# Moving a block's last transpose and its stores behind the next block's first two seed sums on VectorE

## Chip, cores, metric

One NeuronCore of one Trainium2 chip. The metric is the device time of one execution in microseconds (us), median over the runs; lower is better.

## The reference, cut to what matters

```python
# attention part: a causal convolution of 7 taps along the sequence, weights per head
out = np.einsum('hk,bskhg->bshg', w, x_unf)       # B=8, S=4096, D=192
# MoE part, on x = out as (32768, 192)
h = x @ w_in                                      # (32768, 2048)
g = h * np.clip(h + 3.0, 0.0, 6.0) / 6.0
return (g @ w_out).astype(np.float32)             # (32768, 192)
```

## The kernel before

The tokens are worked in 32 blocks of 1024. Both matmuls are done by a Strassen scheme (7 products in place of 8) with float32 operands. Blocks 1 to 31 each have an *h phase* (y times w_in, line 311) and an *out phase* (g times w_out, L422 before, L427 after the change). Matmuls are queued without a break between the two. In the h phase, two independent units L and U run side by side in rows 0 to 63 and 64 to 127 of the array ("halves" below). A list of steps, PLAN, says in which order one pair of units and the pair before it are worked; an apostrophe marks the pair before.

```python
    PLAN = """
        LP1 LRd' UP1 LGd' LP4' UP4' URd' LF1 LP5 UGd' UF1 UP5 LP6 UP6 LP2 LCE UCE LRb'
        UK11 LAF UAF LK11 URb' UP2 LP7 LGb' UP7 LK12 UP3 UGb' LAD LP3 LRa URa LRf UK12
        UAD UGa LGa LK22 UK22 URf LGf UGf LK21 UK21
    """.split()
    # ... in Unit.run(op): P*, K* are matmuls; R is a relu on ScalarE; G a gate on VectorE
            elif op == "F1":                       # ScalarE: bank b starts as a copy of a
                bank["b"] = take()
                nc.scalar.copy(out=psum[:, bank["b"]], in_=psum[:, bank["a"]])
            elif op == "CE":                       # ScalarE: product 5 to SBUF
                self.p5 = p5s.tile([P, N], F32, name="p5")
                nc.scalar.copy(out=self.p5[:], in_=psum[:, bank["e"]])
                give(bank["e"])
            elif op in ("AF", "AD"):               # VectorE: the "seed sums", L391
                to = bank[op[1].lower()] = take()
                nc.vector.tensor_tensor(
                    out=psum[:, to], in0=psum[:, bank["b"]], in1=self.p5[:], op=ALU.add
                )
```

AF reads bank b after product P6 has been added to it, and P7 is added to the same bank afterwards. So P7 has to wait for AF. The out phase ends with sums on VectorE, each followed by a transpose and stores:

```python
        # ... end of out_strassen(i, conv)
        b, bank = three(3, 5, 2)
        piece(p5, 2, bank, NQ)                     # ScalarE copy
        add(u2[:], u2[:], bank[m])                 # VectorE
        give(b)
        add(u2[:], u2[:], p5[:])
        store(i, u2, 0, 1)                         # VectorE transpose, three stores on SyncE
        add(u3[:], u3[:], p5[:])
        store(i, u3, 1, 1)
        # ... main loop: h_phase(); out_strassen(i, ...); x_tiles[i + 2] = load_x(i + 2)
```

Of the kernel before, what the change touches and what calls it, by code (L numbers as in the profile page):

```python
# [16 lines left out]
def kernel(  # L17
# [33 lines left out]
    K3 = D // D2  # L51
# [197 lines left out]
    def conv_units(i, parts, cuts=1):  # L249


        x = x_tiles.pop(i)
        W = N // cuts

        def tap(part, k, t):
            c = c_sb[:, k : k + 1]
            to = y[:, part, t : t + W]
            if k == 0:
                nc.vector.tensor_scalar(  # L259
                    out=to, in0=x[:, part, t : t + W], scalar1=c, scalar2=None, op0=ALU.mult  # L260
                )
            else:
                nc.vector.scalar_tensor_tensor(  # L263
                    out=to, in0=x[:, part, k + t : k + t + W], scalar=c, in1=to,
                    op0=ALU.mult, op1=ALU.add,
                )

        return [
            lambda part=part, k=k, t=t: tap(part, k, t)
            for part in parts for k in range(KC) for t in range(0, N, W)  # L270
        ]
# [28 lines left out]
    def give(b):  # L300
        free_banks.append(b)
# [32 lines left out]
    def h_out(c, group, bs, between):  # L334
# [10 lines left out]



    PLAN = """
        LP1 LRd' UP1 LGd' LP4' UP4' URd' LF1 LP5 UGd' UF1 UP5 LP6 UP6 LP2 LCE UCE LRb'
        UK11 LAF UAF LK11 URb' UP2 LP7 LGb' UP7 LK12 UP3 UGb' LAD LP3 LRa URa LRf UK12  # L350
        UAD UGa LGa LK22 UK22 URf LGf UGf LK21 UK21
    """.split()

# [46 lines left out]
                gate(g_of(2 * u + c, group, k), self.r6[op[1]][:], psum[:, b])  # L400
                give(b)

    def h_phase():
        last = None
        for u in range(UNITS + 1):
            now = [Unit(u, k) for k in range(2)] if u < UNITS else None
            for step in PLAN:
                which = last if step[-1] == "'" else now
                if which:
                    which["LU".index(step[0])].run(step[1:].rstrip("'"))  # L410
            if last:
                g_sums(nc.gpsimd, (1, 3), range(2 * u - 2, 2 * u), 2)
            last = now
# [58 lines left out]
    def g_sums(engine, which, slots, width):  # L472

        forms = {
            1: (S1, A21, A22, ALU.add), 3: (S3, A11, A21, ALU.subtract),
            2: (S2, S1, A11, ALU.subtract), 4: (S4, A12, S2, ALU.subtract),
        }
# [50 lines left out]
    def store(i, c, k, half_, qs=range(NQ), queues=(nc.sync,)):  # L528

        xt = ot.tile([P, N], F32, name="xt")  # L530
        r = slice(qs[0] * QS, (qs[-1] + 1) * QS)
        nc.vector.transpose(out=xt[r], in_=c[r])  # L532
        for q in qs:
            store_rows(i, k, half_ * NQ + q, xt, q, queues[q % len(queues)])
# [46 lines left out]
    def out_strassen(i, conv):  # L581
        p1, p2, p4, p5, u2, u3 = sums_tiles()
        for u in conv:
            u()
        b, bank = three(1, 2, 0)
        nc.scalar.copy(out=p1[:], in_=bank[m])  # L586
        piece(p2, 0, bank, NQ)
        give(b)
        g_sums(nc.vector, (2,), every, 4)
        b, bank = three(4, 2, 1)  # L590
        nc.scalar.copy(out=p4[:], in_=bank[m])  # L591
        piece(p2, 1, bank, NQ)
        give(b)
        swap(slice(0, K3))
        b, bank = by_quarters(2, 2)
        pieces(p2, 2, bank)
        give(b)
        g_sums(nc.vector, (4,), every, 4)
        add(p2[:], p1[:], p2[:])
        store(i, p2, 0, 0)  # L600
        b7, bank7 = three(7, 5, 0)
        piece(p5, 0, bank7, NQ)
        y_sums()
        b, bank = three(6, 5, 1)
        piece(p5, 1, bank, NQ)
        add(u2[:], p1[:], bank[m])
        give(b)
        add(u3[:], u2[:], bank7[m])
        give(b7)
        add(p4[:], u3[:], p4[:], ALU.subtract)  # L610
        store(i, p4, 1, 0)
        b, bank = three(3, 5, 2)
        piece(p5, 2, bank, NQ)
        add(u2[:], u2[:], bank[m])
        give(b)
        add(u2[:], u2[:], p5[:])
        store(i, u2, 0, 1)
        add(u3[:], u3[:], p5[:])
        store(i, u3, 1, 1)

    def split(n):
        if n < len(units):
# [15 lines left out]
    with tc.manual_schedule():  # L638
        nc.vector.tensor_reduce(out=sm[:], in_=e_sb[:], axis=AX.X, op=ALU.add)
        nc.vector.tensor_scalar_add(sm[:], sm[:], 1e-9)  # L640
        nc.vector.reciprocal(sm[:], sm[:])
        nc.vector.tensor_tensor(
            out=c_sb[:], in0=e_sb[:], in1=sm[:].to_broadcast([P, KC]), op=ALU.mult
        )

        thirds = [slice(s, s + 1) for s in range(K3)]
        pe_third = K3 - 1
        b = take()
        for _ in range(3):

            nc.tensor.matmul(
                out=psum[:, b], lhsT=zeros[:, 0:P], rhs=zeros[:], start=True, stop=True
            )
        for k in range(KC):
            nc.scalar.mul(diag[:, k], ident[:], c_sb[:, k : k + 1])
            nc.tensor.matmul(
                out=psum[:, b], lhsT=diag[:, k], rhs=x_tiles[0][:, pe_third, k : k + N],
                start=(k == 0), stop=(k == KC - 1),
            )
        conv0 = conv_units(0, thirds[:pe_third], 2)  # L660
        per = len(conv0) // pe_third
        for k, u in enumerate(conv0):
            if k == 5:
                split(0)
                clamp(0)
            elif k == per - 3:
                join(0, more=False)
            elif k == per:
                nc.scalar.copy(out=y[:, pe_third], in_=psum[:, b])
                give(b)  # L670
                swap(thirds[0])
                swap(thirds[pe_third])
                load(AHEAD)
                split(1)
                clamp(1)
            elif k == per + 6:
                split(2)
                join(1)
                clamp(2)
            u()  # L680
        swap(thirds[1])
        split(3)
        split(4)
        join(2)
        clamp(3)


        parts = [(c, group) for p in range(0, NP, 2) for group in (OWN, OTHER)
                 for c in (p, p + 1)]
        early = [(c, group, (take(), take())) for c, group in parts[:4]]  # L690
        order = (0, pe_third, 1)
        for c in range(2):
            for slot, group, bs in early:
                if slot == c:
                    for s in order[:2]:
                        h_mm(c, group, bs, s, order)
        for c, group, bs in early:
            h_mm(c, group, bs, order[2], order)

        slots = [0, 1, 2, 3, 5, 6, 8, 10, 12, 14]  # L700
        n = 3
        for slot, (c, group) in enumerate(parts):
            first = slot < len(early)
            if first:
                bs = early[slot][2]
            else:
                bs = take(), take()
                for s in range(K3):
                    h_mm(c, group, bs, s)
            more = slot in slots  # L710

            def between():
                if more:
                    join(n)
                    clamp(n + 1)

            if slot == 6:
                x_tiles[1] = load_x(1)
            h_out(c, group, bs, (lambda: None) if first else between)
            if more:  # L720
                split(n + 2)
                if first:
                    between()
                n += 1
        while n < len(units):
            join(n)
            clamp(n + 1)
            split(n + 2)
            n += 1
        w_sums()  # L730
        start_pools.close()
        ss = ctx.enter_context(tc.tile_pool(name="ss", bufs=1))
        p5s = ctx.enter_context(tc.tile_pool(name="p5s", bufs=3))
        cs = ctx.enter_context(tc.tile_pool(name="cs", bufs=1))
        ot = ctx.enter_context(tc.tile_pool(name="ot", bufs=4))

        def conv_and_swap(i):
            return conv_units(i, [slice(0, K3)]) + [lambda: swap(slice(0, K3)), y_sums]

        out_direct(0, conv_and_swap(1))  # L740
        x_tiles[2] = load_x(2)

        S1 = ss.tile([P, NP, N], F32, name="s1")[:]
        for i in range(1, NB):
            h_phase()
            if i + 1 < NB:
                out_strassen(i, conv_units(i + 1, [slice(0, K3)]))
            else:
                out_last(i)
            if i + 2 < NB:  # L750
                x_tiles[i + 2] = load_x(i + 2)
# [33 lines left out]
```

## Time and profile before

| | before |
|---|---|
| time, median (range), 6 runs | 2442.48 us (2442.38 to 2442.60) |
| profiled span | 2440.7 us |
| h phases, first / 23 of them / 7 of them | 38.52 / 39.12 / 39.16 us |
| out phases | 36.19 us |
| transpose of 96x512 on VectorE | 0.708 us, 123 times |

A profile line of a group gives line, engine, operation, shapes and count, then busy time and mean duration in ns, then the engine's idle time ahead of the group and what ended most of it. The waits give who waited for whom: total us, times, longest. The two lines that belong to the seed sums, from the groups of the page and from the list of waits:

```profile
L391 DVE TENSOR_TENSOR psum<-psum,p 128x512 f32<-128x512 f32 x496 | 320.9, 693 | 208.7 <-PE psum L311 204.1
```
```profile
PEld psum L311 <- DVE psum L391: 26.7, 68, 0.6
```

By the first, VectorE mostly waits for TensorE there, not the other way round. The second shows the exceptions: 68 weight loads, about two per block, were released by a seed sum. The rest is read in the prediction.

### The profile page before, as it was taken

The page shows a single profiled execution, that of the slowest core. Times are in us where ns is not written, and L with a number is a line of the kernel's source. Part 1 is how long each engine was busy: PE and PEld are TensorE (multiplying, and loading weights), DVE is VectorE, ACT ScalarE, POOL GpSimd, SP SyncE. Part 2 cuts the span into 40 slices and gives each one's busy share as a digit, 9 for nine tenths or more (in the row PEclk, how much of TensorE's full clock was granted, in tenths as well). Part 3 has the DMA queues.
Part 4 walks back from the last instruction along what each step waited for, and adds up shares of the span by engine and source line. Part 5 has one row for each costly group of instructions (what it writes and reads, how often), then busy time and mean ns, then how long its engine had stood idle before and what let it go on. Part 6 is the DMA issues. An engine that isn't in the chain of part 4 may idle for free.

```text
span 2440.7 us, 40261 instructions
## 1 busy us (share of the span) xinstructions
PE 2430.1 (100%) x16468; PEld 1282.7 (53%) x16468; DVE 2091.1 (86%) x2534; ACT 1083.5 (44%) x1827; POOL 671.4 (28%) x280
## 2 busy tenths in 40 slices
PE   9999999999999999999999999999999999999998
PEld 4335554455554455544555445555455554455544
DVE  8798888898888888888888898888898888888886
ACT  7234553345443355433454334543345443355433
POOL 2523322233311333122332123322233312333122
PEclk9999999999999999999999999999999999999999
DMA  5211122201122111221112211122201122111210
GB/s 143 40 29 26 26 40 40 40 17 30 33 40 40 21 33 27 40 40 24 30 27 40 40 33 23 24 40 40 40 17 35 28 40 40 21 33 27 40 27 14
DMA packets 227338, 84.67 MB, mean 35 GB/s; under 512 B 205456, under 2 KB 210576, under 8 KB 227152
## 3 DMA queue, kind: packets, MB, share of 16 engines
q1 hardware_dynamic: 225848, 81.56, 16.8%
q8 instruction: 129, 2.11, 0.4%
q10 hardware_dynamic: 1208, 0.27, 0.1%
q14 instruction: 57, 0.47, 0.1%
q0 software_dynamic: 96, 0.26, 0.0%
HBM read 31.72 MB, written 25.17 MB: 23 GB/s over the span
## 4 chain that ended last, share of the span: by engine, by line
PE 99%; DVE 1%; DMA 0%; issue 0%; ACTq 0%; SPq 0%; DVEq 0%
PE psum L311 51%; PE psum L422 48%; DVE y L263 0%; DMA x<-in_x_dram 0%; DMA y<-y 0%; DVE c L526 0%; ACTq L92 0%; DVE scale L174 0%; DVE y L259 0%; DVE sig L199 0%; DVE scale L195 0%; DVE top L178 0%; DVE xt L532 0%; SPq L276 0%; DVEq L259 0%
## 5 line engine op out<-in xcount | busy, mean ns | idle before, releaser
L422 PE MATMUL psum<-g,w_out 128*32 128x512 f32 x9312 | 1163.6, 592 | 0.0
L311 PE MATMUL psum<-y,w_in 64*128 64x512 f32 x3664 | 980.0, 591 | 2.9 <-DVE y L263 1.7
L422 PEld LDWEIGHTS psum<-g,w_out 128*32 128x32 f32 x9312 | 337.4, 110 | 811.7 <-issue 762.7
L482 POOL TENSOR_TENSOR s<-g 128x1024 f32<-128x1024 f32 x124 | 293.6, 2368 | 1675.4 <-DVE g L321 1631.2
L317 ACT ACTIVATE r<-psum,half 128x512 f32<-128x512 f32 x1024 | 637.5, 688 | 243.8 <-PE psum L311 241.0
L311 PEld LDWEIGHTS psum<-y,w_in 64*128 64x128 f32 x3664 | 615.5, 187 | 192.9 <-issue 68.9
L321 DVE SCALAR_TENSOR_TENSOR g<-r,psum 128x512 f32<-128x512 f32 x1024 | 642.9, 681 | 4.5 <-ACT r L317 1.3
L311 PE MATMUL psum<-y,w_in_t 64*128 64x512 f32 x1984 | 639.2, 595 | 0.0
L422 PE MATMUL psum<-s,w_out 128*32 128x512 f32 x1488 | 638.5, 592 | 0.0
L391 DVE TENSOR_TENSOR psum<-psum,p 128x512 f32<-128x512 f32 x496 | 320.9, 693 | 208.7 <-PE psum L311 204.1
L263 DVE SCALAR_TENSOR_TENSOR y<-x,c_sb,y 128x1536 f32<-128x1536 f32 (+1 forms) x210 | 416.7, 1991 | 6.6
L311 PEld LDWEIGHTS psum<-y,w_in_t 64*128 64x128 f32 x1984 | 336.2, 187 | 137.7 <-issue 28.3
L518 ACT COPY c<-psum 32x512 f32<-32x512 f32 x188 | 108.9, 579 | 600.5 <-PE psum L422 599.8
L482 POOL TENSOR_TENSOR g<-g 128x1024 f32<-128x1024 f32 x124 | 336.7, 2716 | 9.7
L526 DVE TENSOR_TENSOR c<-c,psum 32x512 f32<-32x512 f32 (+1 forms) x187 | 128.1, 685 | 98.9 <-ACT c L518 93.0
L384 ACT COPY psum<-psum 128x512 f32<-128x512 f32 x248 | 138.6, 571 | 64.2 <-PE psum L311 52.1
L387 ACT COPY p<-psum 128x512 f32<-128x512 f32 x248 | 142.0, 587 | 54.8 <-PE psum L311 51.4
L422 PEld LDWEIGHTS psum<-s,w_out 128*32 128x32 f32 x1488 | 162.4, 110 | 1.2 <-issue 1.2
L482 DVE TENSOR_TENSOR g<-s,g 128x2048 f32<-128x2048 f32 x62 | 141.1, 2316 | 2.2 <-PE psum L422 2.2
L482 DVE TENSOR_TENSOR g<-g 128x2048 f32<-128x2048 f32 x62 | 139.4, 2288 | 2.4 <-PE psum L422 1.4
L586 ACT COPY c<-psum 96x512 f32<-96x512 f32 x30 | 17.5, 582 | 191.1 <-PE psum L422 191.1
L591 ACT COPY c<-psum 96x512 f32<-96x512 f32 x30 | 17.5, 583 | 170.0 <-PE psum L422 170.0
(46 smaller groups left out, 433.8 us busy)
## 6 DMA issues: line engine op xcount, KB each, us to landing
out_dram<-xt SPq DMA_DIRECT2D x382, 64.0 KB, 2.0
y<-y SPq DMA_DIRECT2D x62, 384.0 KB, 4.8
x<-in_x_dram SPq DMA_DIRECT2D x55, 388.5 KB, 5.6
stage<-in_moe_w_in_dram SPq DMA_DIRECT2D x16, 192.0 KB, 4.5
stage<-in_moe_w_out_dram SPq DMA_DIRECT2D x8, 384.0 KB, 6.6
x<-in_x_dram SPq DMA_DIRECT2D x7, 384.0 KB, 4.6
y<-y SPq DMA_DIRECT2D x6, 128.0 KB, 2.3
x<-in_x_dram SPq DMA_DIRECT2D x2, 128.0 KB, 4.4
```

Of the source, the lines that this page charges most:

```text
L263: nc.vector.scalar_tensor_tensor(out=to, in0=x[:, part, k + t : k + t + W], scalar=c, in1=to, op0=ALU.mult, op1=ALU.add,)
L311: nc.tensor.matmul(out=psum[:, b], lhsT=w[r], rhs=y[r, third_of_y], start=start, stop=stop, skip_group_check=onto,)
L317: nc.scalar.activation(r6, h, ACT.Relu, bias=half[:], scale=1.0 / 6.0)
L321: nc.vector.scalar_tensor_tensor(out=out, in0=r6, scalar=1.0, in1=h, op0=ALU.min, op1=ALU.mult)
L384: nc.scalar.copy(out=psum[:, bank["b"]], in_=psum[:, bank["a"]])
L387: nc.scalar.copy(out=self.p5[:], in_=psum[:, bank["e"]])
L391: nc.vector.tensor_tensor(out=psum[:, to], in0=psum[:, bank["b"]], in1=self.p5[:], op=ALU.add)
L422: lambda p=p: nc.tensor.matmul(out=bank[j * QS : (j + 1) * QS], lhsT=w_out[:, p, w, cols], rhs=x[:, p], start=(first and p == ps_[0]), sto ...
L482: engine.tensor_tensor(out=o[:, r], in0=a[:, r], in1=b[:, r], op=op)
L518: nc.scalar.copy(out=dst[rows(q)], in_=src[rows(j)])
L526: nc.vector.tensor_tensor(out=out, in0=x, in1=y, op=op)
L586: nc.scalar.copy(out=p1[:], in_=bank[m])
```

## The change

Intent: let the next block's seed sums, which TensorE waits for, go ahead of work that nobody waits for. The call of `store` for the last part is handed to the next h phase, which runs it at a new step X behind the first LAF and UAF.

```diff
-        UK11 LAF UAF LK11 URb' UP2 LP7 LGb' UP7 LK12 UP3 UGb' LAD LP3 LRa URa LRf UK12
+        UK11 LAF UAF LK11 X URb' UP2 LP7 LGb' UP7 LK12 UP3 UGb' LAD LP3 LRa URa LRf UK12
...
-    def h_phase():
+    def h_phase(left):
...
+                if step == "X":
+                    while left:
+                        left.pop(0)()
+                    continue
...
         add(u3[:], u3[:], p5[:])
-        store(i, u3, 1, 1)
+        return [lambda: store(i, u3, 1, 1)]
...
+        left = []
         for i in range(1, NB):
-            h_phase()
+            h_phase(left)
             if i + 1 < NB:
-                out_strassen(i, conv_units(i + 1, [slice(0, K3)]))
+                left = out_strassen(i, conv_units(i + 1, [slice(0, K3)]))
```

## The prediction

> **What bounds the kernel now.** I read the page's part 1 first, then the chain that ended last, the waits, and last the timeline around one block border.
>
> ```profile
> PE 2430.1 (100%) x16468; PEld 1282.7 (53%) x16468; DVE 2091.1 (86%) x2534; ACT 1083.5 (44%) x1827; POOL 671.4 (28%) x280
> ```
>
> TensorE (PE) is covered from end to end, and part 4 of the page gives 99% of the chain to it. That seems to say that nothing done on VectorE (DVE) can matter. The chain in order of time shows that it is not so simple. Its pieces alternate between the phase that makes h (L311) and the phase that multiplies by w_out (L422):
>
> ```profile
> 100.18 38.52 PE psum L311 x176
> 138.69 36.19 PE psum L422 x336
> 174.88 39.12 PE psum L311 x175
> 214.01 36.19 PE psum L422 x336
> 250.19 39.16 PE psum L311 x175
> 289.35 36.19 PE psum L422 x336
> ```
>
> The columns are start, length, and how many records. The first h phase, which does the same 88 matmuls (two records each), takes 38.52 us; every later one takes 39.12 or 39.16. The first differs in what precedes it: it follows the direct output of block 0, which leaves VectorE no sums and no store to finish. So a later h phase loses some 0.6 us to something at its start, and TensorE "busy" hides it, because records overlap: each lasts 589 ns, while in one half of the array the next starts after 429 ns. (An h phase runs two independent units, L and U, in the lower and upper 64 rows. I call them halves.)
>
> The first 6 us of the h phase in the middle of the run, VectorE and then the weight loads:
>
> ```profile
> 1004.08 0.68 DVE L526 TENSOR_TENSOR c<-c,psum 96x512 f32<-96x512 f32 x1 [2.75 <-ACT c L518]
> 1004.80 0.69 DVE L526 TENSOR_TENSOR c<-c,c 96x512 f32<-96x512 f32 x1
> 1005.52 0.71 DVE L532 STREAM_TRANSPOSE xt<-c 96x512 f32<-96x512 f32 x1
> 1006.15 0.65 DVE L526 TENSOR_TENSOR c<-c,c 96x512 f32<-96x512 f32 x1
> 1006.83 0.71 DVE L532 STREAM_TRANSPOSE xt<-c 96x512 f32<-96x512 f32 x1
> 1007.47 1.26 DVE L391 TENSOR_TENSOR psum<-psum,p 128x512 f32<-128x512 f32 x2
> ```
>
> ```profile
> 1005.17 0.29 PEld L311 LDWEIGHTS psum<-y,w_in_t 64*128 64x128 f32 x2 [0.68 <-ACT psum L384]
> 1007.48 0.19 PEld L311 LDWEIGHTS psum<-y,w_in 64*128 64x128 f32 x1 [0.24 <-issue]
> 1008.19 0.29 PEld L311 LDWEIGHTS psum<-y,w_in_t 64*128 64x128 f32 x2 [0.52 <-DVE psum L391]
> 1008.78 0.18 PEld L311 LDWEIGHTS psum<-y,w_in_t 64*128 64x128 f32 x1 [0.30 <-DVE psum L391]
> ```
>
> VectorE runs without a gap from 1004.08 to 1008.73: the last sums, two transposes, then the two seed sums (L391). The seed sum reads the bank that product P7 accumulates into, so P7 must wait for it. The weight loads of P7 in L and in U stand at 1008.19 and 1008.78, each released by a seed sum. So at this place, though not elsewhere, VectorE is on the path.
>
> **What the Trainium skill says.** "Perfetto Trace Analysis", Identifying the Most-Contended Engine, says that matmul occupancy is a poor measure of the distance to the limit because matmuls are pipelined. This trace agrees: part 1 has 100%, yet one phase of equal work is 0.6 us longer than another. Its section Optimization Strategy advises to find the gaps on the contended engine and the semaphore behind each; that is the step above. "TensorE: Matmul & The Clock Gate", LDWEIGHTS, gives the load time as columns / 1.2 ns, so 107 ns for 128 columns. I use it as an estimate of what a stalled restart adds: a record that starts after a stall lasts 693 ns in place of 589, 104 ns more, and the record after it comes 533 ns later in place of 429. "VectorE: DVE Perf Modes", The DRAIN you can't avoid, has Vector operations run one behind another; here two seed sums take 1.26 us together, which is 0.66 plus 0.60, not less.
>
> **The change, part by part.** In the program order, checked in the built instruction lists: TensorE, ScalarE and GpSimd keep their order exactly. On VectorE the last transpose of a block goes from in front of the next block's first two L391 to behind them, before the third and fourth. On SyncE's queue the three stores of that transpose go behind the next x loads. No instruction is added or removed. It happens at 30 borders: 31 h phases, less the first, which has nothing left over. The last block keeps its own ending.
>
> *Removed from the path.* The transpose, 0.71 us, no longer stands ahead of the seed sums. Can they start earlier by all of it? Three things have to be ready. VectorE is free when the sum before is done, at 1006.15 + 0.65 = 1006.80. The two p copies on ScalarE (L387) end at about 1006.22 and 1006.71. The TensorE records that fill the two seed banks (P6) end at 1006.29 and 1006.78. So the first can start where the transpose started, 1006.83, and end at about 1007.50; the pair ends at 1006.83 + 1.26 = 1008.09 in place of 1008.73. The seed sums gain 0.64.
>
> *When P7 is due.* Reading single TensorE records with the 429 ns cadence: L's last record before P7 starts at 1007.42, so P7 is due in L at 1007.85; it came at 1008.19, late by 0.34. U's last record before starts at 1007.91, so P7 is due in U at 1008.34; it came at 1008.79, late by 0.45. Each then pays 0.104 for the restart. L loses 0.44, U loses 0.55. The h phase ends with U, so the loss at the border is 0.55 us.
>
> *After the change.* L: seed sum done 1007.50, due 1007.85, margin 0.35. U: done 1008.09, due 1008.34, margin 0.25. A release reaches the weight load some 0.05 us after the sum's end (1008.73 to 1008.78), and an uncovered load costs about 0.105, together 0.16, under both margins. So neither should stall, and the whole 0.55 is won.
>
> *A check from the trace itself.* The first h phase has no stall at P7 (its seed sums end at 3.76 and 4.36 us from the phase's start, against 4.80 and 5.40 later on). It is 39.12 - 38.515 = 0.608 shorter. Of this, 0.056 comes earlier, at P6 in U, which waits for a copy on ScalarE (2.271 us against 2.327 from the phase's start), and the change does not touch it. That leaves 0.552. The two ways agree.
>
> *What is added.* The transpose now stands before the third and fourth L391 (which seed the other sum, after P7). VectorE idles 0.62 us there now, waiting for P7. After: seed sums end 1008.09, transpose ends at about 1008.80; P7 in L, now 0.44 earlier, ends at about 1008.87. The transpose fits into the wait, with 0.1 us to spare, and its consumers come many records later. Further on VectorE waits for TensorE by 2 us before the next unit's seed sums, so a shift of 0.55 finds room. The stores leave about 1.3 us later, with 75 us until their buffer is used again.
>
> *The sum.* 30 x 0.552 = 16.6 us. Seven of the 30 phases are the longer ones (39.16: a 73 ns memset of x runs on VectorE ahead of the seed sums, which is then 0.035 later); there the stall is 0.035 longer and goes too if the margin holds: 7 x 0.035 = 0.2. Then 2442.5 - 16.8 = 2425.7 us, 0.7% less. h phases should read 38.57.
>
> **The rivals.** *TensorE is full, so nothing moves:* part 1 at 100% and only 4 us of TensorE waits in the list of waits speak for it; the unequal lengths of equal phases speak against. It would give 2442. *A part of the stall stays in U:* if the weight load must be finished well before its matmul, a margin of 0.25 is thin, since release 0.05 plus the 0.19 us that a load's record lasts make 0.24. Then U may still pay up to the restart of 0.1 per border: 30 x 0.45 = 13.5, so 2429. If the seven memset phases alone pay it, 2426.5. *The displaced transpose delays what it now precedes:* the third and fourth L391 come late, so gates come late, and banks come free late. The 0.1 us of slack is thin but what follows has far more; I count at most 0.1 us per border, 2429. *The stores behind the x loads:* the x loads wait for VectorE's convolution of the same block, long done by then, so the queue does not block; no change. *A new wait on ScalarE's copies:* they end 0.1 us or more before the seed sums want them; no change.
>
> **Range and chances.** I expect 2425.7. The lower end is full removal with a few tens of ns per border more, from halves that fall in better step: 2423.5. The upper end is half of the gain lost to a residual restart: 2433. Faster by over 2% would need 2393.7, that is 49 us, and all that the h phases lose over their bare cadence is 39.12 - 88 x 0.429 = 1.37 us each, 42 us in all; so 1%. Slower by over 2% needs a hazard that I do not see: 1%.
>
> **What would show it.** Right: h phases of 38.57 us in the chain; P7's loads with the ordinary 0.24 gap and no 693 ns record there; seed sums from 3.43 to 4.69 us of the phase instead of 4.14 to 5.40; the transpose between the two pairs; the stall at P6 unchanged; L422 phases still 36.19. A record of 693 ns left at P7 in U alone would show the first partial rival; third and fourth seed sums no earlier than before, the second. I am wrong if h phases stay at 39.12 while the seed sums move, for then they did not hold P7.

## The result, and the profile after

2425.68 us (median of 6 runs, 2425.64 to 2425.81) against 2442.48: 16.80 us less, ratio 0.9931 (95% interval 0.9919 to 0.9944). The difference of 16.8 us is far outside the spread of either.

The chain in order of time (start, us, what), first pieces:

```profile
100.17 38.52 PE psum L311 x176
138.68 36.19 PE psum L427 x336
174.87 38.57 PE psum L311 x175
213.44 36.19 PE psum L427 x336
249.63 38.57 PE psum L311 x175
```

The h phases behind the first are 38.57 us, all thirty of them, and the former 39.16 ones are no longer told apart. The out phases are unchanged. Now the border that was shown before; the first matmul record of its h phase starts here at 997.14 on the profile's clock (before: 1003.33). That is what "the phase's start" means below; the pieces of the chain are put 0.07 us later. VectorE:

```profile
999.97 0.65 DVE L531 TENSOR_TENSOR c<-c,c 96x512 f32<-96x512 f32 x1
1000.53 1.28 DVE L392 TENSOR_TENSOR psum<-psum,p 128x512 f32<-128x512 f32 x2
1001.73 0.69 DVE L537 STREAM_TRANSPOSE xt<-c 96x512 f32<-96x512 f32 x1
1002.71 1.30 DVE L392 TENSOR_TENSOR psum<-psum,p 128x512 f32<-128x512 f32 x2 [0.29 <-PE psum L311]
```

The seed sums (L392 now) follow the last addition, the transpose comes behind them, and VectorE still idles 0.29 us before the next pair. Weight loads of the same border:

```profile
998.98 0.29 PEld L311 LDWEIGHTS psum<-y,w_in_t 64*128 64x128 f32 x2 [0.68 <-ACT psum L385]
1001.28 0.18 PEld L311 LDWEIGHTS psum<-y,w_in_t 64*128 64x128 f32 x1 [0.23 <-DVE psum L392]
1001.66 0.40 PEld L311 LDWEIGHTS psum<-y,w_in_t 64*128 64x128 f32 x2 [0.18 <-issue]
```

The last line merges two loads: L's second one of P7, and U's first. Alone (a narrower window), the latter reads:

```profile
1001.87 0.18 PEld L311 LDWEIGHTS psum<-y,w_in_t 64*128 64x128 f32 x1
```

So both loads of P7 still follow their seed sums by 0.05 us (L's at 4.14 us of the phase, U's at 4.73), but both now come early: P7 starts on time, at 4.52 in L and 5.01 in U, with ordinary records of 589 ns. The loss at P6, which ScalarE's copy releases (first line), is as before. Part 1 of the page:

```profile
PE 2413.0 (100%) x16468; PEld 1042.4 (43%) x16468; DVE 2088.9 (86%) x2534; ACT 1066.5 (44%) x1827; POOL 669.4 (28%) x280
```

A trap for the reader: PEld's busy time fell from 1282.7 to 1042.4 us with the same 16468 loads of the same length (their single times add up to 2246.9 us in both). The halves now run 0.06 us apart, before 0.17, so their loads overlap more and the union is shorter. No load became cheaper.

### The profile page after: what moved, and what is told of

It is laid out like the page before. It is cut to its first block, busy times and chain, and to the rows that moved or that the text cites. A ratio compares the mean times of both kernels' runs of the same rounds, so it can differ in the third digit from the quotient of the medians.

```text
span 2423.9 us, 40261 instructions
## 1 busy us (share of the span) xinstructions
PE 2413.0 (100%) x16468; PEld 1042.4 (43%) x16468; DVE 2088.9 (86%) x2534; ACT 1066.5 (44%) x1827; POOL 669.4 (28%) x280
## 4 chain that ended last, share of the span: by engine, by line
PE 99%; DVE 1%; DMA 0%; issue 0%; ACTq 0%; SPq 0%; DVEq 0%
PE psum L311 51%; PE psum L427 48%; DVE y L263 0%; DMA x<-in_x_dram 0%; DMA y<-y 0%; DVE c L531 0%; ACTq L92 0%; DVE scale L174 0%; DVE y L259 0%; DVE scale L195 0%; DVE sig L199 0%; DVE top L178 0%; DVE xt L537 0%; SPq L276 0%; DVEq L259 0%
## 5 line engine op out<-in xcount | busy, mean ns | idle before, releaser
L311 PE MATMUL psum<-y,w_in 64*128 64x512 f32 x3664 | 957.2, 591 | 3.1 <-DVE y L263 1.7
L321 DVE SCALAR_TENSOR_TENSOR g<-r,psum 128x512 f32<-128x512 f32 x1024 | 643.1, 681 | 4.4 <-ACT r L317 1.1
L311 PEld LDWEIGHTS psum<-y,w_in 64*128 64x128 f32 x3664 | 476.8, 187 | 345.0 <-issue 327.9
L311 PE MATMUL psum<-y,w_in_t 64*128 64x512 f32 x1984 | 610.2, 592 | 0.0
L392 DVE TENSOR_TENSOR psum<-psum,p 128x512 f32<-128x512 f32 x496 | 321.5, 694 | 198.7 <-PE psum L311 194.0
L311 PEld LDWEIGHTS psum<-y,w_in_t 64*128 64x128 f32 x1984 | 280.1, 187 | 209.2 <-issue 142.4
L388 ACT COPY p<-psum 128x512 f32<-128x512 f32 x248 | 135.0, 587 | 61.8 <-PE psum L311 61.1
L385 ACT COPY psum<-psum 128x512 f32<-128x512 f32 x248 | 131.4, 571 | 62.3 <-PE psum L311 56.7
```

The costliest lines, as they stand in the source:

```text
L311: nc.tensor.matmul(out=psum[:, b], lhsT=w[r], rhs=y[r, third_of_y], start=start, stop=stop, skip_group_check=onto,)
L321: nc.vector.scalar_tensor_tensor(out=out, in0=r6, scalar=1.0, in1=h, op0=ALU.min, op1=ALU.mult)
L392: nc.vector.tensor_tensor(out=psum[:, to], in0=psum[:, bank["b"]], in1=self.p5[:], op=ALU.add)
```

## The experiments

Nine kernels, all correct, each timed in three rounds beside the kernel before. The figures "from the phase's start" are read from single records of the traces and are the same in every undisturbed block to 0.01 us.

**1. Only the stores late.** The transpose stays in its old place; its three stores are issued behind the x loads.

```diff
-        return [lambda: store(i, u3, 1, 1)]
+        xt = ot.tile([P, N], F32, name="xt")
+        nc.vector.transpose(out=xt[0:DH], in_=u3[:])
+        return [lambda q=q: store_rows(i, 1, NQ + q, xt, q) for q in range(NQ)]
```

> The last transpose stands where it stood before the change; only its three stores are issued late, behind the x loads, as in the changed kernel. Theory (the transpose ahead of the seed sums holds P7 back): no gain, h phases 39.12 us, time 2442.5. Rival (the gain comes from the order of x loads and stores on SyncE's queue): 2425.7, h phases 38.57.

Measured: 2442.35 us against 2442.36, ratio 1.0 (0.9985 to 1.0015). Its chain:

```profile
1003.33 39.12 PE psum L311 x175
```

The order on SyncE's queue by itself is worth nothing. The gain comes with VectorE's order.

**2. The transpose between the two seed sums.** L's sum is early, U's is not.

```diff
-        UK11 LAF UAF LK11 X URb' UP2 ...
+        UK11 LAF X UAF LK11 URb' UP2 ...
```

> The transpose goes between the two seed sums: L's seed sum is early, U's is not. Theory: the end of the h phase is set by U, whose P7 still comes late, so almost nothing is won. U's seed sum should end about 5.31 us into the phase (0.08 sooner than before the change, since the transpose no longer waits for the addition just ahead of it), P7 in U starts at 5.36 in place of 5.01 and pays 0.10 more, so the phase is about 39.03 and the time 2439.5. Rival (each half carries its own share of the gain): about half the gain, 2434.

Measured: 2438.66 us, ratio 0.9985 (0.9970 to 1.0). VectorE, and the load of P7 in U, at a border whose phase starts at 1001.86:

```profile
1005.25 0.69 DVE L392 TENSOR_TENSOR psum<-psum,p 128x512 f32<-128x512 f32 x1
1005.85 0.69 DVE L537 STREAM_TRANSPOSE xt<-c 96x512 f32<-96x512 f32 x1
1006.47 0.66 DVE L392 TENSOR_TENSOR psum<-psum,p 128x512 f32<-128x512 f32 x1
```
```profile
1007.19 0.18 PEld L311 LDWEIGHTS psum<-y,w_in_t 64*128 64x128 f32 x1 [0.62 <-DVE psum L392]
```

The phase is 39.00 us (expected 39.03). With L's seed sum as early as in the changed kernel and U's 0.12 us earlier than before, 0.12 of the 0.55 is won. U sets the end; rival "each half its share" (2434) falls.

**3 and 4. A delay put back in two sizes.** The changed kernel with a memset on VectorE ahead of the first seed sum of the 30 blocks, 128x300 (measured 0.308 us) and 128x512 (0.485 us).

```diff
             for step in PLAN:
+                if step == "LAF" and left:
+                    nc.vector.memset(dose[:, 0:300], 0.0)    # and 0:512
```

> The changed kernel with a memset of 128x300 on VectorE (about 0.31 us) ahead of the first seed sums of the 30 blocks. Theory: the seed sum of U ends 4.68 us into the phase, is due 5.01, and has to be there about 0.16 sooner, so a delay of 0.25 loses only what passes the margin, about 0.08 a border: 2428. Rival (every delay of the seed sums lengthens the phase one to one): 30 x 0.25 = 7.5 more, 2433.

> The same with 128x512 (about 0.485 us): U's seed sum ends about 5.10, P7's load starts at 5.15 uncovered, a record of 693 ns is back in U, loss about 0.25 a border: h phases 38.82, 2433. Rival (one to one): 30 x 0.42 = 12.6 more, 2438.

Measured: 2429.74 and 2436.38 us, ratios 0.9948 and 0.9975; phases of 38.70 and 38.92. Both lost more than expected (2428 and 2433), and the larger one lies nearer to its rival (2438). The reason is that the memsets delayed U's sum by 0.297 and 0.518 us and not by 0.25 and 0.42: I had taken a memset to hide part of itself behind the addition before it. The border with the larger one (phase from 1001.10), VectorE and U's load of P7:

```profile
1003.92 0.65 DVE L533 TENSOR_TENSOR c<-c,c 96x512 f32<-96x512 f32 x1
1004.63 0.48 DVE L410 MEMSET dose<- 128x512 f32 x1
1005.03 1.26 DVE L392 TENSOR_TENSOR psum<-psum,p 128x512 f32<-128x512 f32 x2
```
```profile
1006.35 0.18 PEld L311 LDWEIGHTS psum<-y,w_in_t 64*128 64x128 f32 x1 [0.30 <-DVE psum L392]
```

With the delays as measured, the "one to one" rival would have 30 x 0.297 = 8.9 and 30 x 0.518 = 15.5 us over the changed kernel; measured are 4.1 and 10.7. Most of the first 0.3 us is free, the rest is not: a margin, as the theory has it. The table under "Why the prediction was right" shows the law.

The smaller memset also shows a stall in part, in the other half. L's seed sum ends 4.381 us into the phase there, 0.135 before L's P7 is due (4.516). P7's load and first record in L (phase from 998.63):

```profile
1003.07 0.29 PEld L311 LDWEIGHTS psum<-y,w_in_t 64*128 64x128 f32 x2
1003.15 0.61 PE L311 MATMUL psum<-y,w_in_t 64*128 64x512 f32 x1
```

The record starts on time but lasts 613 ns, 24 more than 589, and the next one in L comes 24 ns late. In the seven phases with the memset of x the sum is 0.095 early, and the same reading gives 62 to 64 ns.

**5. Both last transposes behind the seed sums.**

```diff
-        store(i, u2, 0, 1)
         add(u3[:], u3[:], p5[:])
-        return [lambda: store(i, u3, 1, 1)]
+        return [lambda: store(i, u2, 0, 1), lambda: store(i, u3, 1, 1)]
```

> Both last transposes of a block go behind the first two seed sums, so these can start about 0.4 us sooner still (then bound by ScalarE's copies and P6) and end near 4.25 us of the phase. Theory: P7 no longer waits in the changed kernel, so more margin is worth nothing: h phases 38.57, 2425.7. Rival (each microsecond taken from ahead of the seed sums pays): 30 x 0.4 = 12 less, 2414.

Measured: 2425.68 us, equal to the changed kernel; U's seed sum ends 0.31 us sooner (4.365; 4.25 was expected), and it buys nothing:

```profile
997.22 38.57 PE psum L311 x175
```

The change has taken all that is to be had at P7.

**6. Sums and transposes spread over the first unit.** One sum ahead of the seed sums, one sum with its transpose behind the first two, the third sum with its transpose behind the first two gates.

```diff
-        LP1 ... LF1 LP5 UGd' UF1 UP5 LP6 ... LK11 X URb' ... UAD UGa LGa LK22 ...
+        LP1 ... LF1 LP5 UGd' UF1 X UP5 LP6 ... LK11 X URb' ... UAD UGa LGa X LK22 ...
         # (cut: the list handed over has three parts, and each X runs one of them)
```

> The last sums and both transposes are spread: one sum ahead of the seed sums, a sum and a transpose behind the first two, the last sum and transpose behind the first two gates. ScalarE and TensorE unchanged. Theory: the remaining loss, P6 of U waiting for ScalarE's second copy (2.33 us of the phase), is not VectorE's, so 2425.7 again. Rival (the displaced work delays the gates and with them the banks): over 2428.

Measured: 2453.33 us, ratio 1.0044 (1.0029 to 1.0059): a miss, slower than the kernel before, 27.7 us over the changed one. VectorE between the gates (L321), and the later of two waits of weight loads, 11.8 us into the phase:

```profile
1013.93 1.26 DVE L321 SCALAR_TENSOR_TENSOR g<-r,psum 128x512 f32<-128x512 f32 x2
1015.12 0.67 DVE L531 TENSOR_TENSOR c<-c,c 96x512 f32<-96x512 f32 x1
1015.83 0.71 DVE L537 STREAM_TRANSPOSE xt<-c 96x512 f32<-96x512 f32 x1
1016.46 2.44 DVE L321 SCALAR_TENSOR_TENSOR g<-r,psum 128x512 f32<-128x512 f32 x4
```
```profile
1018.96 0.30 PEld L311 LDWEIGHTS psum<-y,w_in_t 64*128 64x128 f32 x4 [0.90 <-DVE g L321]
```

The rival was right. The second unit takes the PSUM banks that the first unit's gates give back. The four later gates came some 1.3 us late (the next one at 9.33 us of the phase in place of 8.01), the second unit's P5 found no free bank, and the phase became 39.48.

**7. The same, with U's first seed copy on VectorE.**

```diff
-                nc.scalar.copy(out=psum[:, bank["b"]], in_=psum[:, bank["a"]])
+                copy = nc.vector.tensor_copy if u == 0 and k == 1 else nc.scalar.copy
+                copy(out=psum[:, bank["b"]], in_=psum[:, bank["a"]])
```

> The spread order, and the copy that seeds P6 of U in a block's first unit goes from ScalarE, where it stands behind L's copy, to VectorE, which is free there. Theory: the copy ends about 1.85 us into the phase in place of 2.27, P6 of U starts near 1.91 in place of 2.33, and the end of the phase follows: h phases about 38.15, 31 x 0.42 = 13 less than the changed kernel, 2412.7. Rival (U's stall at P6 is covered by L's, or P7 stalls anew, as its seed sums get less margin): 2420 to 2426.

Measured: 2452.81 us, ratio 1.0042. A miss for the same reason as run 6: TensorE waits for banks, so an earlier P6 is swallowed by that wait. Block 1 has the copy but no deferred work. There U's P6 starts at 1.96 us in place of 2.27, and the phase is 38.27 in place of 38.52, so the copy itself works.

**8. The third piece moved to where VectorE idles**, behind six of the first unit's eight gates, just ahead of the second unit's seed sums.

```diff
-        ... UAD UGa LGa X LK22 ...
+        LP1 ... UGd' UF1 X1 UP5 X3 LP6 ...      # X1 in the first unit, X3 in the second
```

> As the first spread order, but the last sum and transpose stand behind all six gates of the first unit, where VectorE idles 2.02 us in the changed kernel, not between the gates. Theory for the loss of the first spread order (its gates of f and d came 1.35 us late, and the next unit's banks with them): the loss is gone, h phases 38.57, 2425.7. Rival (spreading as such costs, or the deferred work collides with the next unit's seed sums, which have 2.0 us for 1.35): some 0.2 or more a border, 2432.

Measured: 2425.60 us, ratio 0.9931, phases 38.57. The loss of run 6 is gone with nothing but this move, which shows its cause: the place between the gates. The rest of the spread is free.

**9. Run 8 with the copy of run 7.**

> The same with U's first seed copy on VectorE. In the first block of the run with this copy there (which has no deferred work) the phase went from 38.52 to 38.27, since P6 of U started at 1.96 in place of 2.27 and 0.07 to 0.1 was lost again later, at the third unit's P6. Theory: the same here, h phases 38.27 to 38.33, 31 x 0.24 to 0.30 less than the changed kernel: 2416.5 to 2418. Rival (P7 or the next unit stalls anew): 2420 or more.

Measured: 2416.71 us (2416.66 to 2416.86), ratio to the kernel before 0.9895 (0.9880 to 0.9909). It beats both kernels: 9 us less than the changed one, whose ratio was 0.9931 in other rounds, with the kernel before within 0.03 us in both. VectorE at one border, and the chain:

```profile
994.94 0.70 DVE L386 COPY psum<-psum 128x512 f32<-128x512 f32 x1 [2.79 <-PE psum L311]
995.55 0.67 DVE L532 TENSOR_TENSOR c<-c,psum 96x512 f32<-96x512 f32 x1
996.80 1.30 DVE L393 TENSOR_TENSOR psum<-psum,p 128x512 f32<-128x512 f32 x2 [0.58 <-PE psum L311]
```
```profile
993.81 38.27 PE psum L311 x176
```

U's P6 starts 1.96 us into the phase, 0.37 sooner than in the changed kernel; 0.066 is lost again in the third unit, 20.1 us in; the balance, 0.305, is the difference of the phases. Two of the thirty phases (38.55 and 38.44) are longer; why is open.

## Why the prediction was right

Predicted 2425.7, measured 2425.68. Step by step:

*The seed sums hold P7, and U sets the phase's end.* Shown by runs 1 to 5. The cost law of the prediction (P7's start in U less its due time, plus 0.104 for the restart) can be tested on six kernels, in us from the phase's start:

| kernel | U's seed sum ends | U's P7 starts | start - 5.005 + 0.104 | phase - 38.571, measured |
|---|---|---|---|---|
| before | 5.399 | 5.454 | 0.553 | 0.553 |
| transpose between | 5.277 | 5.331 | 0.430 | 0.430 |
| memset 128x512 | 5.197 | 5.251 | 0.350 | 0.350 |
| memset 128x300 | 4.976 | 5.031 | 0.130 | 0.129 |
| changed | 4.679 | 5.005 | none (on time) | 0 |
| both transposes late | 4.365 | 5.006 | none (on time) | 0 |

The four kernels with a late seed sum, late for different reasons, fall on one law to 0.001 us. The first two columns of times show the cause: P7 starts 0.055 after the sum's end, whatever made it late. That the last two columns agree says that nothing later in the phase makes the loss smaller or larger. So a sum should cost nothing if it ends 0.055 + 0.104 = 0.16 us before P7 is due. U alone places that bound only between 0.03 us (the smaller memset, stalled) and 0.32 (the changed kernel's phases with the memset of x, not stalled). L's P7 under the smaller memset settles it: ended 0.135 and 0.095 early, the sums should cost 0.159 - 0.135 = 0.024 and 0.064 us, and they cost 0.024 and 0.062 to 0.064.

*The sum.* 23 phases of 39.124 and 7 of 39.159 became 38.571: 23 x 0.553 + 7 x 0.588 = 16.8 us, which is what the times show. The check against the first phase (0.552 expected) was as good as the arithmetic, since that phase is an unstalled copy of the same work.

*The seed sums' new place* is where I was off. The text's own numbers (1006.83 to 1008.09, phase from 1003.33) are 3.50 to 4.76 us from the phase's start. The line that says 3.43 to 4.69 took the chain's 1003.40 as origin, and that slip hid most of the error, by luck: measured are 3.39 to 4.68. The sums start 0.11 earlier than worked out, because I put the seed sum where the transpose had started, as if VectorE's operations ran strictly one behind the other. The transpose needs the result of the addition ahead of it and starts 0.034 us after its record ends; the seed sum does not and starts 0.076 before it ends. The transpose itself, in its new place behind sums that it does not read, starts 0.087 before the end of the last one. The pair took 1.285 us in place of 1.26, so it ends only 0.08 earlier than predicted, and U's margin was 0.33, not 0.25. The seven phases with the memset of x, at 4.689, do not stall either.

*The transpose in the wait before the third and fourth seed sum.* It was predicted to leave 0.1 us (0.07 by the times given); the profile after has 0.29. Of the 0.22 between, 0.08 is the earlier end of the seed sums, 0.09 is that the transpose starts ahead of the last one's recorded end, 0.02 is its shorter record, and 0.03 passes from the end of P7's record to the third seed sum.

*The rivals.* "TensorE is full, so nothing moves" fell. "A part of the stall stays in U" took 0.24 us as the earliness that P7 may need; L under the smaller memset shows 0.16, so by the law a margin of 0.25 would have done too. "The displaced transpose delays what follows" did not happen here (the third seed sum starts 5.57 us into the phase, 6.02 before), but run 6 shows that it was no idle fear: the same kind of work a few steps later, between the gates, costs 0.9 us per border. "Stores behind the x loads" is worth nothing (run 1). Better step of the halves (0.06 us apart in place of 0.17) gave nothing beyond the 0.55, so the low end of the range had no ground.

## What to carry to other kernels

An engine that shows 100% can still lose time at one place in every round; compare stretches that do the same work, and the one without the neighbour tells the size of the loss before anything is changed. Ask of each consumer when it is due, and move work that nobody waits for behind the work it delays, into a wait of the same engine; beyond the margin that the consumer needs (0.16 us here), more earliness is worth nothing. Before work is moved, look at what the operations behind its new place give back (here PSUM banks): a sum and a transpose between the gates cost 0.9 us per block, the same two behind them cost nothing.

## What the Trainium skill lacked or had wrong

- "TensorE: Matmul & The Clock Gate", LDWEIGHTS, has columns / 1.2 ns. For float32 the records here last 187 ns for 128 columns and 110 ns for 32, where the formula has 107 and 27. The added time of a stalled restart, 104 ns (693 against 589), is near the formula's 107 for 128 columns; that the two are the same thing is not shown.
- No page that I read gives this restart cost, or the release: a weight load that waits for a VectorE result starts 0.05 us after that record's end, and unless it came early its matmul's first record is up to 104 ns longer. A result 0.32 us ahead of the due time cost nothing here, one 0.135 ahead cost 0.024.
- "VectorE: DVE Perf Modes", The DRAIN you can't avoid, has the next operation start when the pipe is empty, and sends the reader on for the exceptions. In these records a seed sum that does not need the result ahead of it starts 0.076 us before the end of that record, and a transpose that does need it starts 0.034 after. A margin worked out from a profile needs this difference of 0.11 us; no section states it as a time. The need of a result is not all of it: the memsets of runs 3 and 4, which need nothing from the addition ahead, start 0.016 and 0.06 after its record ends; why is open.
- "Perfetto Trace Analysis", Identifying the Most-Contended Engine, offers the LDWEIGHTS busy share, the sum of the loads' times over the window, for TensorE. That is 92% before and 93% after (2246.9 us in both). The profile page's PEld share, which counts loads that overlap once, fell from 53% to 43% because the two halves came into step. The section does not say that loads can overlap, as they do here, and that the two ways of counting then differ.
